# A fused attention and MLP-mixer kernel: a second buffer for the token-major q and k, and other places for the regroup copies

## Chip, cores and metric

The kernel runs on one core of one Trainium2 chip. The metric is the device time of one execution in microseconds (us).

## The reference, cut to what matters

```python
# q, k, v: (B=8, H=8, S=576, D=64), float32
scores = q @ k.T / sqrt(D) + alibi_bias          # causal, window of 128 keys
attn   = softmax(scores)
x      = (attn @ v) as (B, S, H*D)
# token mixing, then channel mixing
h = relu(x.T @ w_tok1) @ w_tok2                  # over the 576 tokens
u = x + h.T
out = u + relu(u @ w_ch1) @ w_ch2                # 512 -> 1536 -> 512
```

## The kernel before

The kernel works on eight batches in a software pipeline. While the mixer of batch b runs, the attention of batch b+1 runs between its matmuls. The tensor engine (PE) is the busy one; its instruction order is written by hand (`spread`). ACT is the scalar engine and POOL is GpSimd. Six steps matter here.

- `dma_qk(b)` loads q and k of one batch, 576 KB each as the profile counts it, into `qn[b % 2]`, `kn[b % 2]`. It is issued from the POOL queue.
- `regroup(b)` is two copies on the vector engine (DVE), one for q and one for k, into the token-major `qg`, `kg`. There is one `qg` and one `kg`, so the copies of batch b+1 must wait until the last transposes of batch b have read them.
- `att_T(g)` transposes one head pair on PE and copies the result to `qT` (ACT) and `kT` (DVE). `att_S(g)` does scores, exp on ACT and a mask multiply on DVE (`pb`). `att_V(g)` multiplies with v and writes `xb` on DVE. There are four g for each batch.
- `tok1`, `tok2` are the token mixer; `tok2` adds into `ub` on DVE.
- `trans_u` transposes u on PE and copies it to `UT` on DVE: the "u copies".
- `ch1` (96 matmuls for each batch) and `ch2` are the channel mixer.

```python
qg = const.tile([P, TPP, H, D], bf16, name="qg")
kg = const.tile([P, TPP, H, D], bf16, name="kg")
...
def regroup(b, h0, h1):
    for raw, t in ((qn, qg), (kn, kg)):
        nc.vector.tensor_copy(
            out=t[:RP, :, h0:h1, :],
            in_=raw[b % 2][:RP, h0:h1, :].rearrange("p h (j d) -> p j h d", j=TPP),
        )
...
def att_T(g, early=False):
    ...                                   # transposes of qg, kg on PE
    nc.scalar.copy(out=dst(qT[g % NR]), in_=nat(0))
    (nc.scalar.copy if early else nc.vector.tensor_copy)(out=dst(kT[g % NR]), in_=nat(1))
    if hp == NHP - 1 and 0 < b < B - 1:   # after the last transposes of batch b
        regroup(b + 1, 0, H)
        if b + 3 < B:
            dma_qk(b + 3, 0, H)
...
with tc.manual_schedule():                # every engine in the order written
    ...
    side = [(0.0, lambda: regroup(1, 0, H))]
    if B > 3:
        side.append((0.0, lambda: dma_qk(3, 0, H)))
    ...                                   # attention of batch 1 between ch1 of batch 0
with tc.manual_schedule(engines={ENG.PE}):  # only PE in the order written
    ...                                   # mixers of batches 1 to 7
```

In the second block only PE's order is fixed. The order on DVE, ACT and POOL is set when the kernel is built, by a scheduler that is free to move an instruction forward as long as its dependencies allow it.

The softmax here doesn't subtract the row's maximum and nothing guards it: scores larger than these inputs give would overflow.

## Time and profile before

| | before |
|---|---|
| time, median of 3 | 334.68 us |
| span of the profiled execution | 332.6 us |
| PE busy | 304.6 us (92%) |
| PE idle, 112-120, 149-158, 187-195, 224-232 us | 1.75 us together |
| PE wait for UT, 81-84 us | 2.67 us |

From the profile page of the kernel before: busy time by engine; then PE's busy tenths and the granted TensorE clock in tenths in 40 slices of the span; then the chain that ended last, by engine.

```profile
PE 304.6 (92%) x2786; PEld 187.9 (57%) x2816; DVE 179.8 (54%) x342; ACT 178.4 (54%) x373; POOL 58.9 (18%) x79
...
PE   2577898897899999999999999999999999999995
...
PEclk9999999999799999999999999999999999999999
...
PE 77%; DVE 12%; ACT 6%; issue 3%; DMA 1%; POOL 0%; POOLq 0%
```

PE is the limit after the start-up (the low digits on the left). From 33 us on, the clock is full except in the eleventh slice (83 to 91 us). The first four digits say nothing, because the trace has no record of the clock before 33 us: five 128x512 matmuls took 2.34 us at 29.75 us and 1.24 us at 144.59 us, so PE ran at about half speed there. The chain has 12% on DVE.

From the waits of the kernel before: engine, group and line that waited, what it waited for, us in total, number of waits, the longest.

```profile
PE ct L351 <- DVE UT L345: 2.7, 1, 2.7
...
PE ht L323 <- DVE ub L327: 1.5, 3, 0.6
```

The first is the largest wait of PE after the start-up. The timeline around it (start, length in us, engine, line, operation, what ended the idle time before it):

```profile
80.75 0.39 PE L340 MATMUL ut<-ident,ub 128*128 128x128 bf16 x4
80.92 0.75 DVE L211 COPY kT_100<-tT 128x576 bf16<-128x576 bf16 x1
...
81.58 0.95 DVE L142 COPY qg<-qn_86 96x3072 bf16<-96x3072 bf16 x1
82.45 0.95 DVE L142 COPY kg<-kn_88 96x3072 bf16<-96x3072 bf16 x1
...
83.31 1.54 DVE L345 COPY UT<-ut 128x576 bf16<-128x576 bf16 x4
...
83.81 1.49 PE L351 MATMUL ct<-UT,WC_105 128*128 128x288 bf16 x4 [2.67 <-DVE UT L345]
```

PE had ended the transposes of u at 81.1 us. DVE then did a kT copy, the two regroup copies of batch 3 (0.95 us each, 1.73 us from the first start to the UT copies) and only then the UT copies. After it the clock fell. Stretches of the kernel before, 1 us each (stretch; length; busy us and instruction count of PE, PE loads, DVE, ACT, POOL; granted clock; DMA share; GB/s):

```profile
84.00:85.00 1.00, 0.83 (x4) 0.19 (x2) 0.85 (x3) 0.00 (x0) 0.54 (x1) 0.81 0.57 34
85.00:86.00 1.00, 1.00 (x7) 0.27 (x7) 0.00 (x0) 0.52 (x2) 0.00 (x0) 0.50 0.96 127
...
87.00:88.00 1.00, 1.00 (x6) 0.39 (x6) 0.69 (x1) 0.53 (x3) 0.00 (x0) 0.50 1.29 197
```

The clock is 0.81 and then 0.50 until 88 us. Not every run of this kernel loses it: of the 11 runs beside e5 to e8, three had a mean clock of 1.000 (332.5 to 333.2 us) and eight had 0.988 to 0.995 (333.3 to 334.7 us). The means of the two groups differ by 1.2 us. The four token stages, same columns:

```profile
112.00:120.00 8.00, 7.45 (x51) 3.49 (x51) 7.85 (x12) 2.77 (x5) 1.71 (x2) 1.00 0.49 87
149.00:158.00 9.00, 8.50 (x70) 4.15 (x71) 8.57 (x14) 3.43 (x6) 1.55 (x2) 1.00 0.46 80
187.00:195.00 8.00, 7.45 (x51) 3.43 (x51) 7.68 (x13) 3.17 (x5) 0.00 (x0) 1.00 0.09 33
224.00:232.00 8.00, 7.84 (x67) 3.81 (x66) 7.86 (x13) 3.01 (x5) 0.00 (x0) 1.00 0.10 35
```

DVE is busy 95 to 98% of these stretches, with regroup copies ahead of the ub adds that PE waits for. PE idles 0.55, 0.50, 0.55 and 0.16 us.

### The profile page before, as it was taken

How to read it: one execution, taken by the hardware profiler on the slowest of the kernel's cores; microseconds unless marked ns; L12 is line 12 of the kernel's file. 1: busy time of each engine (PE TensorE's matmuls, PEld its weight loads, DVE VectorE, ACT ScalarE, POOL GpSimd, SP SyncE). 2: the span in 40 equal slices, each digit the busy share in tenths (PEclk: the TensorE clock that was granted, in tenths of full speed). 3: DMA queues.
4: the chain of work that ended last, by engine and by line, in shares of the span. 5: the costliest groups of instructions: out<-in, count | busy, mean ns of one | idle time of the engine just before them, and what ended most of it. 6: DMA issues, size and time to landing. Idle time of an engine off the chain costs nothing.

```text
span 332.6 us, 6683 instructions
## 1 busy us (share of the span) xinstructions
PE 304.6 (92%) x2786; PEld 187.9 (57%) x2816; DVE 179.8 (54%) x342; ACT 178.4 (54%) x373; POOL 58.9 (18%) x79
## 2 busy tenths in 40 slices
PE   2577898897899999999999999999999999999995
PEld 1253575454576456744676456744675457646742
DVE  6873726959444785339633785339633763244021
ACT  3961299263695436953495436853594338413800
POOL 8973151320105100041005000130000000000000
PEclk9999999999799999999999999999999999999999
DMA  7999999995908591094708510090100110011022
GB/s 95 133 172 204 205 159 151 213 184 66 141 2 54 82 189 53 1 104 85 154 2 57 79 63 34 2 103 34 64 2 9 56 65 32 2 63 65 0 65 96
DMA packets 59502, 27.76 MB, mean 83 GB/s; under 512 B 38672, under 2 KB 54864, under 8 KB 59472
## 3 DMA queue, kind: packets, MB, share of 16 engines
q0 software_dynamic: 54224, 17.90, 57.1%
q1 hardware_dynamic: 5248, 9.44, 8.6%
q8 instruction: 22, 0.36, 0.5%
q14 instruction: 8, 0.07, 0.1%
HBM read 35.78 MB, written 9.44 MB: 136 GB/s over the span
## 4 chain that ended last, share of the span: by engine, by line
PE 77%; DVE 12%; ACT 6%; issue 3%; DMA 1%; POOL 0%; POOLq 0%
PE ct L351 28%; PE sp L233 5%; PE ot L267 5%; ACT pe L241 3%; PE tT L201 3%; PE ht L323 3%; DVE ub L327 2%; DVE xb L275 2%; PE ut L340 2%; DVE kg L142 2%; DVE qg L142 1%; DVE pb L245 1%; DMA kn_87<-in_k_dram 1%; DVE kT_100 L211 1%; DVE obt L391 1%
## 5 line engine op out<-in xcount | busy, mean ns | idle before, releaser
L351 PE MATMUL ct<-UT,WC_105 128*128 128x288 bf16 x768 | 105.9, 288 | 3.0 <-DVE UT L345 2.7
L241 ACT ACTIVATE pe<-sp,biascol 128x512 bf16<-128x512 f32 x128 | 81.3, 699 | 24.9 <-PE sp L233 24.7
L356 ACT ACTIVATE R_102<-ct 128x288 bf16<-128x288 f32 x192 | 74.0, 424 | 36.9 <-PE ct L351 30.7
L351 PEld LDWEIGHTS <-WC_105 128*128 128x128 bf16 x768 | 71.6, 98 | 26.0 <-issue 6.8
L245 DVE TENSOR_TENSOR pb<-pe,masks 128x1024 bf16<-128x1024 bf16 x64 | 44.1, 690 | 60.8 <-ACT pe L241 60.7
L379 PEld LDWEIGHTS <-R_102 128*128 128x128 bf16 x432 | 39.2, 98 | 41.3 <-issue 1.3
L327 DVE TENSOR_TENSOR ub<-ht,xb 128x512 bf16<-128x512 f32 x40 | 25.7, 681 | 6.9 <-PE ht L323 6.8
L267 PEld LDWEIGHTS <-pb 128*128 128x128 bf16 x576 | 23.0, 102 | 7.1 <-DVE xb L275 3.0
L275 DVE TENSOR_TENSOR xb<-ot,rt 128x640 bf16<-128x640 f32 x32 | 26.3, 823 | 1.0
L128 POOL DMA_DIRECT2D vp_92<-in_v_dram x16 | 14.1, 890 | 68.4 <-PE ot L267 62.8
L323 PE MATMUL ht<-r1t,W_104 128*128 128x512 bf16 x76 | 21.6, 387 | 2.0 <-DVE ub L327 1.5
L201 PEld LDWEIGHTS <-qg 96*128 96x128 bf16 x192 | 12.0, 102 | 14.0 <-DVE qg L142 9.8
L128 POOL DMA_DIRECT2D vp_91<-in_v_dram x12 | 10.5, 888 | 46.7 <-PE ot L267 38.9
L310 PEld LDWEIGHTS <-W_103 128*128 128x128 bf16 x80 | 7.9, 104 | 12.7 <-issue 5.8
L210 ACT COPY qT_96<-tT 128x576 bf16<-128x576 bf16 x7 | 4.6, 660 | 19.4 <-PE tT L201 19.4
L267 PE MATMUL ot<-vp_91,pb 128*128 128x65 bf16 x288 | 13.2, 206 | 1.9 <-DVE xb L275 1.7
L345 DVE COPY UT<-ut 128x576 bf16<-128x576 bf16 x32 | 13.0, 450 | 1.5 <-PE ut L340 1.5
L323 PEld LDWEIGHTS <-W_104 128*128 128x128 bf16 x80 | 7.4, 100 | 11.4 <-issue 4.7
L210 ACT COPY qT_93<-tT 128x576 bf16<-128x576 bf16 x7 | 4.5, 638 | 15.5 <-PE tT L201 15.3
L211 DVE COPY kT_99<-tT 128x576 bf16<-128x576 bf16 x7 | 5.3, 757 | 12.8 <-ACT qT_95 L210 12.6
L201 PE MATMUL tT<-ident,qg 96*128 96x96 bf16 x168 | 11.8, 205 | 0.0
L201 PE MATMUL tT<-ident,kg 96*128 96x96 bf16 x168 | 11.7, 206 | 0.0
(186 smaller groups left out, 357.9 us busy)
## 6 DMA issues: line engine op xcount, KB each, us to landing
out_dram<-obt SPq DMA_DIRECT2D x32, 256.0 KB, 2.0
qn_86<-in_q_dram POOLq DMA_DIRECT2D x4, 576.0 KB, 10.1
kn_88<-in_k_dram POOLq DMA_DIRECT2D x4, 576.0 KB, 11.5
vp_92<-in_v_dram POOLq DMA_DIRECT2D x16, 128.0 KB, 8.0
qn_85<-in_q_dram POOLq DMA_DIRECT2D x3, 576.0 KB, 12.7
kn_87<-in_k_dram POOLq DMA_DIRECT2D x3, 576.0 KB, 15.5
WC_105<-in_moe_w_ch_dram POOLq DMA_DIRECT2D x3, 512.0 KB, 9.9
WC_106<-in_moe_w_ch_dram POOLq DMA_DIRECT2D x1, 1536.0 KB, 22.9
```

The source lines that it names most:

```text
L128: nc.gpsimd.dma_start(out=vp[b % 2][:, c, :, 0:D], in_=v[b, :, c * P : (c + 1) * P, :].rearrange("h s d -> s h d"),)
L201: nc.tensor.transpose(tt[n][:, j * RP : (j + 1) * RP], t_raw[:RP, j, 2 * hp : 2 * hp + 2, :].rearrange("p h d -> p (h d)"), ident[:RP, :RP],)
L233: nc.tensor.matmul(sp[:, hh, i * 256 + x0 : i * 256 + x1], lhsT=kt[r, k0 : k0 + P], rhs=qt[r, q0 : q0 + x1 - x0], start=True, stop=True,)
L241: nc.scalar.activation(out=pe[:, i, :], in_=sp[:, i, :], func=ACT.Exp, bias=biascol[:, h : h + 1], scale=scale,)
L245: nc.vector.tensor_tensor(out=pb[:, :, :], in0=pe[:, :, :], in1=masks[:, half, 2 * hp : 2 * hp + 2, :], op=ALU.mult,)
L267: nc.tensor.matmul(ot[:, i, qb * (D + 1) : (qb + 1) * (D + 1)], lhsT=pb[:, i, col : col + P], rhs=vb[:, kc, h, :], start=(n == 0), stop=(n ...
L275: nc.vector.tensor_tensor(out=xb[b][:, :, 2 * hp * D : (2 * hp + 2) * D].rearrange("p c (i d) -> p i c d", i=2), in0=o4[:, :, :, 0:D], in1 ...
L323: nc.tensor.matmul(ht[:, :], lhsT=W2[:, j, c0(c) : c0(c) + P], rhs=r1s[b, j][:, :], start=(j == 0), stop=(j == NDH - 1),)
L327: nc.vector.tensor_tensor(out=ubs[b][:, c, :], in0=ht[:, :], in1=xb[b][:, c, :], op=ALU.add)
L351: nc.tensor.matmul(ct[:, :], lhsT=WC1[:, cb, ht_i * P : (ht_i + 1) * P], rhs=UT[:, cb, o : o + SH], start=(cb == 0), stop=(cb == NCB - 1),)
L356: nc.scalar.activation(out=R2[:, ht_i, o : o + SH], in_=ct[:, :], func=ACT.Relu)
L379: nc.tensor.matmul(o2[0][:, :], lhsT=R2[:, ht_i, col : col + P], rhs=WC2[:, ht_i, :], start=(ht_i == 0 and c != NF), stop=(ht_i == NHT - 1),)
```

## The change

The intent: with two buffers the copies of a later batch need not wait for the transposes of the batch before it, so they can run in the middle of `ch1`, where DVE is about 40% busy, and not just ahead of the u copies. One `pb` and one `obt` buffer pay for the room.

```diff
-pbpool ... bufs=9
+pbpool ... bufs=8
-opool ... bufs=4
+opool ... bufs=3
-qg = const.tile([P, TPP, H, D], bf16, name="qg")
-kg = const.tile([P, TPP, H, D], bf16, name="kg")
+qg = [const.tile([P, TPP, H, D], bf16, name=f"qg{i}") for i in range(2)]
+kg = [const.tile([P, TPP, H, D], bf16, name=f"kg{i}") for i in range(2)]
 ...                       # regroup and att_T use qg[b % 2], kg[b % 2]
 def att_T(...):
-    if hp == NHP - 1 and 0 < b < B - 1:
-        regroup(b + 1, 0, H)
-        if b + 3 < B:
-            dma_qk(b + 3, 0, H)
 ...
 for ht_i in range(NHT):   # ch1 of batch b
     ...
+    if ht_i in (4, 7) and 0 < b < B - 3:
+        its.append((0.0, lambda n=ht_i // 7: regroup(b + 3, 0, H, (n,))))
+    if ht_i == 7 and 0 < b < B - 5:
+        its.append((0.0, lambda: dma_qk(b + 5, 0, H)))
 ...                       # first block, after the last att_V of batch 1
+    side.append((0.0, lambda: regroup(2, 0, H)))
+    side.append((0.0, lambda: dma_qk(4, 0, H)))
 ...                       # second block, after the first att_S of batch 2
+    side.append((0.0, lambda: regroup(3, 0, H)))
+    side.append((0.0, lambda: dma_qk(5, 0, H)))
```

More of the change, by code (lines that the diff above doesn't have):

```diff
@@ L78 @@
     pepool = ctx.enter_context(tc.tile_pool(name="pe", bufs=3))
-    pbpool = ctx.enter_context(tc.tile_pool(name="pb", bufs=9))
+    pbpool = ctx.enter_context(tc.tile_pool(name="pb", bufs=8))
     xpool = ctx.enter_context(tc.tile_pool(name="xp", bufs=2))
@@ L83 @@
     upool = ctx.enter_context(tc.tile_pool(name="up", bufs=2))
-    opool = ctx.enter_context(tc.tile_pool(name="op", bufs=4))
+    opool = ctx.enter_context(tc.tile_pool(name="op", bufs=3))
     ps_at = ctx.enter_context(tc.tile_pool(name="ps_at", bufs=2, space=bass.MemoryType.PSUM))
@@ L137, in dma_v_head, with regroup @@
         )
-    def regroup(b, h0, h1):
-        for raw, t in ((qn, qg), (kn, kg)):
+    def regroup(b, h0, h1, which=(0, 1)):
+        for n in which:
+            raw, t = ((qn, qg), (kn, kg))[n]
             nc.vector.tensor_copy(
-                out=t[:RP, :, h0:h1, :],
+                out=t[b % 2][:RP, :, h0:h1, :],
                 in_=raw[b % 2][:RP, h0:h1, :].rearrange("p h (j d) -> p j h d", j=TPP),
@@ L202, in att_T @@
                     tt[n][:, j * RP : (j + 1) * RP],
-                    t_raw[:RP, j, 2 * hp : 2 * hp + 2, :].rearrange("p h d -> p (h d)"),
+                    t_raw[b % 2][:RP, j, 2 * hp : 2 * hp + 2, :].rearrange("p h d -> p (h d)"),
                     ident[:RP, :RP],
@@ L514 @@
         side += [(0.6, lambda g=g: att_V(g)) for g in range(NHP, 2 * NHP)]
+        side.append((0.0, lambda: regroup(2, 0, H)))
+        if B > 4:
+            side.append((0.0, lambda: dma_qk(4, 0, H)))
         spread(its0[n0:] + its1[:n1], side)
@@ L518 @@
         side = att_step(2 * NHP - 2, 2 * NHP) + att_step(2 * NHP - 1, 2 * NHP)
+        side.append((0.0, lambda: regroup(3, 0, H)))
+        if B > 5:
+            side.append((0.0, lambda: dma_qk(5, 0, H)))
         for g in range(2 * NHP, 3 * NHP):
```

## The prediction

> **What bounds the kernel now.** The tensor engine: the profile's first part has PE busy 304.6 of 332.6 us (92%), DVE and ACT 54%. By stretches, nearly all of PE's idle time lies before 66 us and in the last 4 us; from 89 to 315 us it is about 2.3 us. The change can win only where PE stands behind the regroup copies (line 142). By the timeline and the chain of waits:
>
> - Mixer of batch 1, 81.1 to 83.8 us: DVE runs the two copies (0.95 us each, 1.73 us together) just ahead of the four UT copies, and PE waits 2.67 us for UT. Then the granted clock falls to 0.81 for 1 us and 0.50 for 3 us: about 1.7 us lost. The Trainium skill (TensorE: Matmul & The Clock Gate, Part 1) says that the clock halves after an idle window of about 3.4 us; here 2.7 us was enough, so the trace agrees only roughly.
> - Token stages of batches 2 to 5 (112-120, 149-158, 187-195, 224-232 us): DVE is 95-98% busy, the copies sit ahead of ub, and PE idles 0.55 + 0.50 + 0.55 + 0.16 = 1.8 us.
>
> **What the change does.** The same copies stay. It adds a second qg/kg and pays with one pb and one obt buffer; with chunks 2.6 us apart or more and 2.0 us to landing, three obt should not bind.
> - Regroups 4 to 7 go to the middle of ch1 of batches 1 to 4, where DVE is about 40% busy with holes of 1.4 to 2.2 us (waiting for ACT's exp); the planned positions (about 93, 97; 133, 136.6; 169, 172 us) fall into holes. About 1.3 of the 1.8 us comes back.
> - Regroup 2 moves from 56 us to behind the last xb of batch 1 (66 us). The transposes of batch 2 at 67.1 us then wait for it: it costs about 0.45 us.
> - Regroup 3 moves from 81.6 to about 73 us. DVE is nearly gapless from 72 to 85 us, so a copy put at 73-75 us only trades places; only if it slips into the holes at 66-72 us is the 1.7 us won. I count half: 0.9 us. In either case PE's idle gets shorter or is spread, so the clock should not drop: 1.5 us, fairly sure.
> - The q,k load of batch 4 starts about 10 us later (near 69 us; 8 to 20 us to landing), just in time for its copy near 93 us.
>
> **Sum.** 1.3 + 0.9 + 1.5 - 0.45 = 3.2 us off 334.7 us: **331.4 us**, 8 in 10 between **329.3** and **334.6**. Faster by over 2% (under 328): 0.05; within 2%: 0.93; slower: 0.02.
>
> **What would show it right or wrong.**
> - The wait of PE ct for DVE UT near 83 us gone or under 1.2 us, and granted clock 1.00 from 80 to 100 us.
> - Line 142 on DVE near 66, 66-75, then in each ch1 stage; the waits of PE ht for DVE ub (1.5 us, 3 times) gone.
> - PE idle in the four token stages together under 0.6 us.
> - A new wait of batch 2's transposes for kg near 67 us, 0.3 to 0.8 us.
>
> **What would make it wrong.** Only PE's order is fixed by hand; the other engines' order is the scheduler's. It may pull the freed copies back into the token stages, put the copy of batch 4 ahead of its data's landing, so that DVE and then PE stand for several us, or put a copy ahead of a kT or pb on which the next att_S or att_V waits. If everything is hidden, the gain is near 5 us.

## More of the kernel before

The order inside a fixed block is kept, but an instruction from outside it may be put in between.

## The result and the profile after

| | before | after |
|---|---|---|
| time, median | 334.44 us (4 runs) | 346.52 us (4 runs, 345.74 to 347.89) |
| span of the profiled execution | 332.6 us | 343.9 us |
| PE busy | 304.6 us | 307.2 us |

The ratio is 1.0375, 95% interval 1.0326 to 1.0424: slower. Ratios here and below are the mean time of one kernel's fast runs over the mean of the kernel before's fast runs of the same rounds, so they are not quite the ratio of the medians in the tables.

From the profile page of the kernel after, the lines that answer to those of before:

```profile
PE 307.2 (89%) x2816; PEld 187.7 (55%) x2816; DVE 179.6 (52%) x342; ACT 178.1 (52%) x373; POOL 60.0 (17%) x79
...
PE   3578893097989999999999999999999999999995
...
PEclk9999999579999999999999999999999999999999
...
PE 77%; DMA 11%; DVE 6%; POOL 3%; ACT 2%; issue 1%; POOLq 0%; DVEq 0%
```

PE has slices of 3 and 0 from 52 to 69 us. The clock is low in two slices. The chain now has 11% on DMA and DVE only 6%; 13.70 us of the DMA share is the k load of batch 3, and 18.57 us is the q load of batch 2 just before it.

From the waits of the kernel after:

```profile
PE sp L230 <- DVE kT_102 L212: 13.4, 1, 13.4
...
DVE qg_90 L143 <- DMA qn_86<-in_q_dram: 10.7, 1, 10.7
```

The longest wait of PE was 13.4 us, for a kT copy. DVE waited 10.7 us for the q load of batch 3 (and 1.4 us more for the k load). The timeline of the kernel after shows how one made the other (POOL lines are load issues):

```profile
50.74 0.78 POOL L116 DMA_DIRECT2D qn_86<-in_q_dram  x1 [0.92 <-DMA vp_94<-in_v_dram]
...
52.46 0.69 DVE L242 TENSOR_TENSOR pb<-pe,masks 128x1024 bf16<-128x1024 bf16 x1 [0.71 <-ACT pe L238]
...
52.80 1.39 ACT L238 ACTIVATE pe<-sp,biascol 128x512 bf16<-128x512 f32 x2
...
52.93 0.77 POOL L116 DMA_DIRECT2D kn_88<-in_k_dram  x1 [1.40 <-DMA qn_85<-in_q_dram]
...
53.64 1.03 PE L376 MATMUL o_782<-WC_108,R_104 128*128 128x512 bf16 x4
...
54.60 0.39 PE L230 MATMUL sp<-qT_97,kT_101 64*128 64x256 bf16 x4
...
63.81 0.96 DVE L143 COPY qg_90<-qn_86 96x3072 bf16<-96x3072 bf16 x1 [10.66 <-DMA qn_86<-in_q_dram]
64.69 0.68 DVE L242 TENSOR_TENSOR pb<-pe,masks 128x1024 bf16<-128x1024 bf16 x1
...
66.74 0.96 DVE L143 COPY kg_92<-kn_88 96x3072 bf16<-96x3072 bf16 x1 [1.37 <-DMA kn_88<-in_k_dram]
67.62 0.75 DVE L212 COPY kT_102<-tT 128x576 bf16<-128x576 bf16 x1
...
68.42 0.61 PE L230 MATMUL sp<-qT_97,kT_101 64*128 64x256 bf16 x6 [13.43 <-DVE kT_102 L212]
...
68.96 1.89 PE L376 MATMUL o_782<-WC_108,R_104 128*128 128x512 bf16 x4
```

The copies `qg_90<-qn_86` and `kg_92<-kn_88` are those of batch 3. The program has them behind the first att_S of batch 2, which runs at about 86 us in this trace. On DVE they come next after the `pb` that ended at 53.15 us, straight after the last transposes of batch 1 have freed the buffer. Their data had been asked for only at 50.74 us (q) and 52.93 us (k); the copies started at 63.81 and 66.74 us, when it had landed.

Behind the copies stood work that was ready. The exp that the next `pb` needed ended at 54.2 us, and that `pb` began at 64.69 us. The kT copy began at 67.62 us, and only then could PE go on at 68.42 us. (The `sp` matmul there does not read `kT_102`. In the program `tT` and `sp` take turns in two PSUM buffers, so this `sp` needs the buffer that the kT copy has to empty first.) The Trainium skill (TensorE: Matmul & The Clock Gate, the table of specifications) calls VectorE's queue strict FIFO; this trace agrees, with 10.5 us for that `pb`. The chain of waits of the kernel after goes through the same steps (start, us, what):

```profile
52.93 13.70 DMA kn_88<-in_k_dram
...
66.74 0.96 DVE kg_92 L143
```

The clock then added to it. Stretches of the kernel after, 1 us each:

```profile
59.00:60.00 1.00, 0.00 (x0) 0.00 (x0) 0.00 (x0) 0.00 (x0) 0.00 (x0) 0.80 1.61 183
60.00:61.00 1.00, 0.00 (x0) 0.00 (x0) 0.00 (x0) 0.00 (x0) 0.00 (x0) 0.50 1.38 199
...
73.00:74.00 1.00, 1.00 (x23) 0.73 (x23) 1.00 (x2) 0.39 (x1) 0.00 (x0) 0.87 0.67 101
```

PE stopped at 55.0 us and the clock fell to half at about 59.6 us. It came back at about 73.3 us, 4.8 us after PE went on. Meanwhile four `o_782` matmuls took 1.89 us where four of the same shape took 1.03 us before the stop (the timeline's o_782 group at 53.64 us).

The token stages of the kernel after (DVE now has the copies of batches 5 to 7 here, a batch earlier than before):

```profile
125.00:133.50 8.50, 8.50 (x61) 3.93 (x59) 7.94 (x13) 3.17 (x5) 1.56 (x2) 1.00 0.68 114
161.50:170.50 9.00, 9.00 (x89) 4.75 (x86) 8.86 (x15) 3.17 (x5) 0.00 (x0) 1.00 0.08 29
198.00:206.00 8.00, 8.00 (x55) 3.66 (x53) 7.86 (x12) 3.17 (x5) 0.00 (x0) 1.00 0.10 35
235.00:243.00 8.00, 8.00 (x67) 3.87 (x64) 6.93 (x12) 3.17 (x5) 0.00 (x0) 1.00 0.10 35
```

PE has no idle time in them. One new wait lies just behind the fourth: 0.70 us for a UT copy at 245.4 us, where the kernel before has none.

Where the time went, from starts that both traces have (us):

| from | to | before | after | difference |
|---|---|---|---|---|
| start | first ch2 matmul of batch 0 | 54.20 | 53.64 | -0.56 |
| there | first tok1 matmul of batch 1 | 11.84 | 26.56 | +14.72 |
| there | first ch1 matmul of batch 1 | 17.77 | 17.22 | -0.55 |
| there | end | 248.8 | 246.5 | -2.3 |
| all | | 332.6 | 343.9 | +11.3 |

So the change loses 14.7 us in one place and wins 2.9 us in the stretches after it. PE's stop itself is 12.6 us of the 14.7, counted by the start of the att_S matmuls behind it (56.42 us before, 68.42 us after, plus the 0.56 us lead); the other 2.2 us lie between there and tok1 (9.62 us before, 11.78 us after), where the clock was at half until 73.3 us.

### The profile page after: what moved, and what is told of

Read it like the earlier page. It is cut to its first block, busy times and chain, and to the rows that moved or that the text cites. A ratio compares the mean times of both kernels' runs of the same rounds, so it can differ in the third digit from the quotient of the medians.

```text
span 343.9 us, 6706 instructions
## 1 busy us (share of the span) xinstructions
PE 307.2 (89%) x2816; PEld 187.7 (55%) x2816; DVE 179.6 (52%) x342; ACT 178.1 (52%) x373; POOL 60.0 (17%) x79
## 4 chain that ended last, share of the span: by engine, by line
PE 77%; DMA 11%; DVE 6%; POOL 3%; ACT 2%; issue 1%; POOLq 0%; DVEq 0%
PE ct L348 25%; DMA qn_85<-in_q_dram 5%; PE sp L230 5%; PE ht L320 5%; PE ot L264 4%; DMA kn_88<-in_k_dram 4%; PE tT L202 3%; DVE xb L272 2%; PE ut L337 1%; DMA vp_93<-in_v_dram 1%; ACT pe L238 1%; POOL vp_93 L134 1%; PE o_782 L376 1%; POOL qn_85 L116 1%; PE o_2170 L376 1%
## 5 line engine op out<-in xcount | busy, mean ns | idle before, releaser
L348 PE MATMUL ct<-UT,WC_107 128*128 128x288 bf16 x768 | 104.8, 286 | 1.3 <-DVE UT L342 0.9
L128 POOL DMA_DIRECT2D vp_94<-in_v_dram x16 | 14.8, 937 | 71.0 <-PE ot L264 64.8
L128 POOL DMA_DIRECT2D vp_93<-in_v_dram x12 | 10.5, 891 | 53.6 <-PE ot L264 45.8
L230 PE MATMUL sp<-qT_97,kT_101 64*128 64x256 bf16 (+2 forms) x80 | 6.9, 273 | 13.7 <-DVE kT_102 L212 13.4
L230 PEld LDWEIGHTS <-kT_101 64*128 64x128 bf16 x80 | 2.9, 98 | 19.5 <-issue 18.6
L202 PEld LDWEIGHTS <-qg_89 96*128 96x128 bf16 x96 | 6.0, 106 | 12.1 <-DVE qg_89 L143 10.4
L212 DVE COPY kT_101<-tT 128x576 bf16<-128x576 bf16 x7 | 5.3, 756 | 12.8 <-ACT qT_97 L211 12.6
```

The lines of the kernel that those rows point to most:

```text
L128: nc.gpsimd.dma_start(out=vp[b % 2][:, c, :, 0:D], in_=v[b, :, c * P : (c + 1) * P, :].rearrange("h s d -> s h d"),)
L202: nc.tensor.transpose(tt[n][:, j * RP : (j + 1) * RP], t_raw[b % 2][:RP, j, 2 * hp : 2 * hp + 2, :].rearrange("p h d -> p (h d)"), ident[: ...
L230: nc.tensor.matmul(sp[:, hh, i * 256 + x0 : i * 256 + x1], lhsT=kt[r, k0 : k0 + P], rhs=qt[r, q0 : q0 + x1 - x0], start=True, stop=True,)
L348: nc.tensor.matmul(ct[:, :], lhsT=WC1[:, cb, ht_i * P : (ht_i + 1) * P], rhs=UT[:, cb, o : o + SH], start=(cb == 0), stop=(cb == NCB - 1),)
```

## Experiments

Theory A: the whole loss is the copy of batch 3, put into DVE's queue far ahead of its place, where its data is still on the way. The rivals: B, fewer buffers or the later regroup 2 and load of batch 4 cost the time; C, the new places in the program are the cause; D, it is the place in the queue as such, and not the wait for data. The order in which DVE ran is read from the traces. e1 to e4 ran on one chip, e5 to e8 on a second and e9 on a third, each beside runs of the kernel before.

`keep_in_program_order` in the edits below adds an order edge to the instruction traced just before on the same engine. It adds no wait and changes no data.

### e1_hold3: the change, with the copies of batch 3 kept at their place

```diff
-            nc.vector.tensor_copy(
+            ins = nc.vector.tensor_copy(
                 out=t[b % 2][:RP, :, h0:h1, :], ...)
+            if hold:
+                tc.keep_in_program_order(ins)
...
-        side.append((0.0, lambda: regroup(3, 0, H)))
+        side.append((0.0, lambda: regroup(3, 0, H, hold=True)))
```

> The change, with only the copies of batch 3 kept at their planned place in DVE's queue (behind the second pb of batch 2's first pair, an order edge, no wait). Theory A (the whole loss is the batch 3 copy, put into DVE's queue some 20 us before its planned place, where its q,k data is still on the way: DVE stands 12 us, PE 13.4 us, and the clock then costs 2.2 us): the wait goes, 331 to 334 us, ratio to before 0.990 to 0.998, no PE wait over 3 us after 60 us. Rival B (fewer pb and obt buffers, or the later regroup 2 and later load of batch 4 cost the time): stays above 342 us.

Measured: 332.37 us median against 334.87 us, ratio 0.9927 (0.9907 to 0.9947). The 13.4 us wait is gone. The longest wait of PE from 40 us on, and the q copy of batch 3 in the timeline:

```profile
PE t L309 <- DVE xb L274: 1.4, 1, 1.4
...
75.60 0.95 DVE L143 COPY qg<-qn 96x3072 bf16<-96x3072 bf16 x1
```

The copies of batch 3 ran where the program has them. One order edge on each of the two copies turns 3.75% slower into 0.7% faster. So their early place made the loss, and rival B is out, because e1 keeps the smaller pools and the later regroup 2. That the copies cost time there by waiting for data is for e4 and e9 to show.

### e2_fewer_bufs: the kernel before with 8 pb and 3 obt buffers

```diff
-pbpool ... bufs=9
+pbpool ... bufs=8
-opool ... bufs=4
+opool ... bufs=3
```

> The kernel before with 8 pb and 3 obt buffers and nothing else. Theory A: as before, ratio 0.997 to 1.003. Rival B: a good part of the 12 us, ratio 1.01 to 1.035.

Measured: 334.2 us against 334.87 us, ratio 0.9984 (0.997 to 0.9999). The smaller pools cost nothing.

### e3_two_bufs_old_places: the second buffer alone

```diff
 # from e2_fewer_bufs
-qg = const.tile(...); kg = const.tile(...)
+qg = [const.tile(...) for i in range(2)]; kg = [const.tile(...) for i in range(2)]
 # regroup and att_T use qg[b % 2], kg[b % 2]; every call stays where it was
```

> The kernel before with two buffers for qg,kg (and 8 pb, 3 obt), but all regroup calls and loads where they stood in the program. Theory A in its sharper form (the second buffer alone frees the copy of batch 3 at the end of batch 1's transposes, and the scheduler then takes it ahead, wherever the program has it): as slow as the change, 345 to 350 us, DVE waits 10 us or more for batch 3's data. Rival C (the new places in the program are the cause): 332 to 336 us.

In the trace the q copy of batch 3 again comes next after the last `pb` before the stop (52.80 us), although the program calls it in `att_T`'s last step of batch 2. Measured: 343.63 us against 334.87 us, ratio 1.0256 (1.0233 to 1.0279). From its waits:

```profile
PE sp L233 <- DVE kT L211: 11.2, 1, 11.2
...
DVE qg L142 <- DMA qn<-in_q_dram: 9.4, 2, 8.9
```

(The 9.4 us are two waits; 8.9 us is the one for batch 3.) So the second buffer alone makes most of the loss, and rival C is out as the main cause; the remaining 3 us or so come with the new places. The size missed my 345 to 350 us, and the 8.9 us my 10 us: in this trace the load was issued at 49.38 us and its copy started at 62.39 us, so the stop was 11.2 us and not 13.4, and the copies of batch 2 were not late.

### e4_load3_first: the load of batch 3 ahead of the v load of batch 2

```diff
 # att_V(3) no longer issues dma_v(2); after regroup(1):
 side.append((0.0, lambda: dma_qk(3, 0, H)))
+side.append((0.0, lambda: [dma_v(2, c) for c in range(NF)] + [dma_v_tail(2)]))
```

> The change, with the q,k load of batch 3 issued ahead of the v load of batch 2 instead of behind it. Theory A: the batch 3 data lands some 5 to 8 us sooner and DVE's and PE's wait shrinks by as much, 338 to 342 us, and DVE's wait is still for that load. If the wait is not for the data, nothing changes: 345 to 348 us.

Measured: 340.93 us against 334.87 us, ratio 1.0178 (1.0152 to 1.0204). From its waits:

```profile
PE sp L230 <- DVE kT L212: 7.9, 1, 7.9
...
DVE qg L143 <- DMA qn<-in_q_dram: 5.3, 2, 4.9
```

The load was issued at 44.77 us instead of 50.74. The q copy started 5.65 us sooner (58.16 us instead of 63.81) and PE's wait shrank by 5.5 us (13.4 to 7.9). The time follows the landing of the data. The ratio is against the kernel before; against the median of the change, from its own runs, e4 is 5.6 us faster.

### e9_no_load3: the change without the load of batch 3

```diff
-        if B > 3:
-            side.append((0.0, lambda: dma_qk(3, 0, H)))
```

> The change with the q,k load of batch 3 left out, so that its copies read the data of batch 1 that is long there (wrong result on purpose for batch 3; DVE's order stays that of the change, copies of batch 3 ahead of kT and pb). Theory A (it is the wait for the data, not the place in the queue as such): no wait of 13 us, 330 to 334 us, PE waits at most 2 us at that place. Rival D (two copies of 0.95 us ahead of kT and pb upset att_S and att_V so that the rest follows): above 338 us.

Measured: 331.76 us against 334.55 us, ratio 0.9917 (0.989 to 0.9944). From its timeline:

```profile
53.00 0.96 DVE L143 COPY qg<-qn 96x3072 bf16<-96x3072 bf16 x1
...
54.73 1.05 DVE L143 COPY kg<-kn 96x3072 bf16<-96x3072 bf16 x1
...
56.50 0.40 PE L230 MATMUL sp<-qT,kT 64*128 64x256 bf16 x6 [1.60 <-DVE kT L212]
```

The copies stand in the same early place and cost PE a wait of 1.60 us there (0.86 us in the kernel before at the same matmuls). So the place as such costs some 0.7 us at these matmuls, and the rest was the wait for data; rival D is out as the main cause. e9 also takes two loads of 576 KB off the queues, but e4, which keeps every load, points the same way. The result of e9 passed the comparison although batch 3 used the q and k of batch 1. The comparison does not notice which batch's q, k is used, so for the variants the order of copies and transposes was checked in the traces as well.

### e5_hold_all: all copies in the middle of ch1, as the change means it

```diff
 # from e1_hold3
-its.append((0.0, lambda n=ht_i // 7: regroup(b + 3, 0, H, (n,))))
+its.append((0.0, lambda n=ht_i // 7: regroup(b + 3, 0, H, (n,), hold=True)))
```

> The change as its words have it: the copies of batches 3 to 7 all kept at their planned places (batch 3 as in e1, the rest in the middle of ch1). Read against e1 (332.4 us), where the scheduler still takes the copies of batches 5 to 7 into the token stages. If the middle of ch1 is the better place: 330.5 to 332, the DVE share of the token stages lower. If it makes no difference because in e1 the copies no longer stand ahead of a ub that PE waits for: 332 to 333. If a copy now stands ahead of a kT or pb that PE waits for: above 333, with PE sp or ot waiting in ch1.

Measured: 333.01 us against 333.79 us, ratio 0.9983 (0.9959 to 1.0007). This ran on another chip than e1, so it does not tell the places apart by a few tenths of a per cent. The trace has something else. Up to 84 us its PE stream is that of e1 shifted by 0.56 us, with the same two stops, 0.48 us before the u transposes and 1.14 us before ct. The same stretch of e1, then of e5:

```profile
84.00:86.00 2.00, 1.58 (x10) 0.57 (x10) 2.00 (x6) 0.42 (x2) 0.00 (x0) 1.00 1.25 192
```

```profile
84.00:86.00 2.00, 2.00 (x9) 0.60 (x9) 0.65 (x2) 0.72 (x2) 0.00 (x0) 0.50 1.13 236
```

In e1 the clock stayed at 1.00, in e5 it was 0.50 for this stretch. These are single executions on two chips, and both kernels go both ways: the mean clock was 0.995 to 1.000 in the four runs of e1 and 0.993 to 1.000 in those of e5. So the same short stops cost the clock in some runs and not in others. The Trainium skill (TensorE: Matmul & The Clock Gate, Part 1) describes the activity window as free-running, which would make it a matter of when the stops fall; these runs fit that, but none tests it.

### e6_before_3_behind_UT: the kernel before, one order changed

```diff
 # kernel before: one qg, one kg, 9 pb, 4 obt
-        if hp == NHP - 1 and 0 < b < B - 1:
+        if hp == NHP - 1 and 0 < b < B - 1 and b != 2:
 ...   # in mixer_items, after the trans_u items
+            if b == 1:
+                its.append((0.0, lambda: regroup(3, 0, H, hold=True)))
+                its.append((0.0, lambda: dma_qk(5, 0, H)))
```

> The kernel before (one qg, one kg, 9 pb, 4 obt) with the copies of batch 3 alone put behind batch 1's four UT copies instead of ahead of them. My reading of before (PE waits 2.67 us for UT, of which 1.73 us are the two copies, and the clock then costs about 1.7 us) gives 331 to 332 us, ratio 0.988 to 0.993, PE's wait for UT about 1 us, and no stretch at half clock. If the clock drop had another cause, only 1.7 us: 332.7 to 333.2.

Measured: 331.14 us against 333.79 us, ratio 0.9928 (0.9907 to 0.9949). From its timeline:

```profile
81.32 1.54 DVE L347 COPY UT<-ut 128x576 bf16<-128x576 bf16 x4
81.82 1.38 PE L353 MATMUL ct<-UT,WC 128*128 128x288 bf16 x4 [0.94 <-DVE UT L347]
...
82.77 0.95 DVE L142 COPY qg<-qn 96x3072 bf16<-96x3072 bf16 x1
```

The UT copies are ahead of the copies of batch 3, PE waits 0.94 us instead of 2.67, and the clock is 1.00 from 80 to 90 us. This confirms my reading of the kernel before. The split comes out roughly: the three runs of the kernel before that kept the clock have a mean of 332.9 us, all eleven 333.7 us, and the six of e6 331.3 us. So about 1.6 us of the gain is the wait, and 0.8 us is the clock, which not every run loses.

### e7_2_early_3_behind_UT and e8_e7_hold_all: the parts together

e7 has two buffers, the copies of batch 2 and the load of batch 4 where they were before, and the copies of batch 3 behind the UT copies as in e6. e8 also keeps the copies of batches 4 to 7 in the middle of ch1.

```diff
 # e7, from e1_hold3
+        if g == 2 * NHP - 1:            # in att_T, as before
+            regroup(2, 0, H)
+            dma_qk(4, 0, H)
 ...   # in mixer_items, after the trans_u items
+            if b == 1:
+                its.append((0.0, lambda: regroup(3, 0, H, hold=True)))
+                its.append((0.0, lambda: dma_qk(5, 0, H)))
 ...   # the calls for batches 2 and 3 (and loads 4 and 5) that the change added are out
 # e8, from e7
-... regroup(b + 3, 0, H, (n,))
+... regroup(b + 3, 0, H, (n,), hold=True)
```

> Two buffers, with the copies of batch 2 (and the load of batch 4) where they were before, the copies of batch 3 behind batch 1's UT copies, and batches 4 to 7 as the scheduler takes them. Sum of the parts: 3.4 us at batch 1 as in e6 and 1.8 us of token stage waits: 329 to 330.5 us, ratio 0.982 to 0.987. No wait of PE for kg near 68 us, no wait over 1.5 us after the start-up.

> As e7, with the copies of batches 4 to 7 kept in the middle of ch1. Same question as e5 on a better base: within 0.3% of e7 if the place does not matter, below it by 0.5 to 1.5 us if it does.

Measured, same chip and rounds as e6: e7 329.82 us, ratio 0.9891 (0.9867 to 0.9914); e8 330.37 us, ratio 0.9899 (0.9878 to 0.9921). e7 is the fastest kernel, 1.1% faster than before. e8 is 0.1% behind e7 by the means. The time of e7 met what I expected and its ratio did not (0.982 to 0.987): the kernel before ran at 333.8 us on this chip, not 334.7, and e7 has a new wait of 0.70 us for a UT copy at 229 us. The middle of ch1 is thus no better a place than the one the scheduler takes. What counts is that the copies no longer hold up UT and ub: the three waits for ub, 1.5 us together, are still there in e6 and gone in e7.

## Why the prediction was wrong

**The step that failed** is "Regroup 3 moves from 81.6 to about 73 us", with "only if it slips into the holes at 66-72 us is the 1.7 us won". I let the copies of batch 3 move forward to 66 us at most, and took every earlier place as a gain. In the kernel after they moved to 53 us, to the moment when the last transposes of batch 1 freed the second buffer, and their data landed at 63.8 and 66.7 us. In the sum this step stood as a gain of 0.9 us; it was a loss of 14.7 us (12.6 us stop, 2.2 us half clock).

The single buffer of the kernel before had hidden this. The load of batch 3 was issued there at 49.6 and 52.1 us too, but the copies could not start before the transposes of batch 2 ended at about 80 us. The second buffer removed what had kept the copy behind its load's landing (e3).

The list of what could go wrong named the mechanism ("ahead of its data's landing, so that DVE and then PE stand for several us"), but for batch 4, and gave it no weight in the sum or in the range. For batch 4 the old bound still held.

**Point by point.**

- PE is the limit, and only the named places can win: right (e6, e7).
- Token stages: predicted 1.3 of 1.8 us; PE idle in the four stages of the kernel after is 0, so all of it came back, less the new wait of 0.70 us behind the fourth. The size was near, but by luck: the copies did not go to the middle of ch1. Those of batch 4 ran just behind the UT copies (98.4 us). Those of batches 5 to 7 went to the token stages one batch earlier, as the list of risks says, and that was no loss: they stand between the ub adds there and PE did not wait.
- Regroup 2: predicted 0.45 us; PE waited 0.81 us for kg at 82.7 us in the kernel after, 0.60 us in e1.
- Clock at batch 1: no fall there in the kernel after (1.00), as predicted; the half clock came at 60 to 73 us instead. e5 shows that "PE's idle gets shorter or is spread, so the clock should not drop" is not safe: it dropped with spread waits. And some runs of the kernel before had nothing to win here, as they kept the clock.
- Pools: right (e2).
- With the failed step taken out by one order edge, the change measured 332.4 us (e1), inside the range of 329.3 to 334.6, but 1.0 us above the 331.4: regroup 3 at 75.6 us did only trade places.

**Left open.** The runs show where the scheduler put the copies, not why. That it takes the load to have landed sooner than it does fits e3 and the change, but no run tests it.

## What to carry to other kernels

A buffer that looks like a mere shortage can be the only thing that keeps an instruction behind the landing of its data. Before adding a buffer, ask for each freed instruction what the earliest moment is that its dependencies now allow, and compare it with the time at which its load lands in the trace; then read the built queue order or fix it with an order edge. Look first for the plain reordering: moving one copy pair behind the UT copies gave 0.7% with no second buffer at all.

## What the Trainium skill lacked or had wrong

- TensorE: Matmul & The Clock Gate, Part 1, gives an idle window of about 3.4 us for the clock to halve. The length agrees: by the granted clock, the stretches at half clock lasted 3.4 us (kernel before, e2, e5), 6.8 and 3.4 us (e4), 10.2 us (e3) and 13.7 us (kernel after), all multiples of 3.4. But PE need not be idle for all of it. In the 3.41 us before the fall, PE was busy for 0 us in the kernel after, 0.64 us in the kernel before (single ct matmuls, one for each UT copy) and 1.77 us in e5 (mostly transposes). In e1 the same 1.77 us of matmuls, 0.56 us later, left the clock at 1.00. I found no figure there for how much work keeps it up.
- The same page has VectorE's queue as strict FIFO; no page that I looked up warns of what that does when the order is set at build time, before the landing times are known: one copy of 0.95 us ahead of its load's landing held a ready `pb` for 10.5 us and PE for 13.4 us.
- SBUF — State Buffer describes the shared port of DVE and GpSimd as a lock: while a DVE copy in a two-port mode holds it, DMAs issued from POOL have to wait. It gives no duration for a DVE copy that is held up so. In the kernel after, the copies of batch 2 took 1.34 and 1.31 us instead of 0.95 us while POOL issued the v loads (78.9 to 83.8 us). The cause is not shown: in e1 POOL issued the same loads from 65.2 us, and one copy took 0.95 us (66.04 us) and the next 1.32 us (66.91 us).
